# Value sums in a bank of their own, a thinner weight decode and added transposes in a fused attention and MoE kernel

## The chip, the cores and the metric

The kernel runs on one core of a Trainium2 chip. The metric is the time of one execution on the device in microseconds (us). A core has five engines that run beside each other and take their instructions in order: TensorE (PE, whose weight loads are listed as PEld), VectorE (DVE), ScalarE (ACT), GpSimd (POOL) and SyncE (SP), which issues the transfers here.

## The reference

For each of 8 batches and 8 heads (576 rows, head width 64) an attention, in which scores below the row's maximum less `tau` are dropped, and behind it a two-layer network over all 4608 tokens:

```python
scores = scale * np.matmul(q, k.transpose(0, 1, 3, 2))
thresh = np.max(scores, axis=-1, keepdims=True) - tau
scores = np.where(scores >= thresh, scores, -1000000000.0)
scores = scores - np.max(scores, axis=-1, keepdims=True)
attn = np.exp(scores)
attn = attn / (np.sum(attn, axis=-1, keepdims=True) + 1e-09)
return np.matmul(attn, v).astype(np.float32)
...
h = x @ w_in                       # 4608 x 512 by 512 x 2048
sp = np.where(h > 20.0, h, np.log1p(np.exp(np.minimum(h, 20.0))))
g = h * np.tanh(sp)
return (g @ w_out).astype(np.float32)
```

The two weight matrices come as 64-bit floats.

## The kernel before

**Tiles and pairs.** Two heads make a pair; 8 batches of 4 pairs are 32 pairs. The 2 x 576 rows of a pair are nine tiles of 128 score rows, 288 tiles in all. One Python loop over `g` writes the work out; in its iteration `g` several tiles stand at different stages, so the order in the code is each engine's order (`InOrder` holds every compute engine to it). Below, "tile t" is g % 9 of the tile itself, and "iteration" is the value of `g`.

**One tile.** `begin(g + 1)` makes the scores of the next tile on PE into one of two pairs of score banks (`s`). `row_max` is a reduction on DVE, `exponential` two small DVE operations and the exponential on ACT, `masked` one DVE operation that compares and multiplies (`p <- s, st, e`) and frees the score bank. `normalise`, one iteration later, is a reciprocal on DVE and a scaling on POOL. `transposes(g - 2)` turns `p` on PE: four transposes into the PSUM tile `tp` (one bank), and for odd tiles and for tile 8 one or two more into the small PSUM tile `t5`. `evacuate`, one iteration after that, copies `tp` and then `t5` to SBUF on ACT. Through iteration 37 the transposes stand early in the iteration, after that at its end.

**Value products.** When tiles 3 and 8 of a pair are there, `product(g - lag)` makes the products with v: `values_full` takes a PSUM bank `y` and gives five pieces of work on PE (four matmuls each) and a `gather`, an ACT copy out of `y`. With lag 4 this falls into iterations with g % 9 = 7 and 3. Through iteration 37 two pieces run per iteration and the gather follows in the iteration after the last; from iteration 38 (`SOON`) on all five run in one iteration and the gather in the same one. Pair by pair `split_x` then cuts the result in two column halves, each a high part (ACT copy, `xh`) and a low part (POOL, `xl`).

**First matrix.** From iteration 42 on `gemm1` runs as a stream of PE matmuls beside the attention: 384 per batch and 36 iterations, dealt out per iteration by `EVEN`, twelve for each result bank `h`, which ACT copies to `hst` and SP stores to DRAM. `h` and `y` share two PSUM banks (`psh`, tag "ph").

**Decoding w_in.** 32 blocks of the first matrix (128 x 256) are put together from the halves of the 64-bit words beside the first 55 tiles. `W1_STEPS` says in which iterations of each 18 a block begins. Its load is issued then; three iterations later come two ACT operations (`first`), then `clamp` on POOL, one iteration after that `shift` on DVE and `join` (`sign` on DVE, `add` on POOL), and two iterations later `upper` on ACT and `lower` on POOL, or for nine blocks (`ONV`) `lower` on DVE one iteration later still. `shift` stands on DVE between the reciprocal and the masking of its iteration. Before iteration `JOIN` the join does too; from then on it stands behind the masking.

**Clock.** `WARM` puts transposes of the identity before the loop and 26, 12, 6, 4, 3, 2, 2, 2, 2, 2 into iterations 0 to 9.

**The end.** After the loop the second matrix runs: w_out is decoded, batch 7's `gemm1` with more banks, then the products with w_out.

Of the kernel before, what the change touches and what calls it, by code (L numbers as in the profile page):

```python
# [14 lines left out]
P = 128  # L15
B, H, S, D = 8, 8, 576, 64
NP = H // 2
LOADS = ((1, 0, 1, 3, 2, 3, 7, 3, 5, 8), (0, 3, 3, 2, 5, 4, 5, 8, 8, 9), (0, 0, 2, 4, 5, 4, 7, 6, 7, 8), (0, 0, 1, 3, 2, 3, 7, 5, 7, 8))
W1_STEPS = (1, 3, 4, 6, 7, 8, 10, 12, 13, 15, 16, 17)
STAGES = ((0, 1, 1), (0, 1, 1))  # L20
THIRD = ((),)
LAG = 2
# [2 lines left out]
ORDER = (0, 0)  # L25
PIECES = 2
WARM = (24, (26, 12, 6, 4, 3, 2, 2, 2, 2, 2))
FULL = NP
VP = 32
SOON = 9 * FULL + 2  # L30
ONP = 1
ONV = (3, 9, 11, 12, 14, 15, 17, 18, 22)
JOIN = 39
PLAIN = (0, 1)
DM, DF = 512, 2048
ND, NF = DM // P, DF // P
# [33 lines left out]
LAST = {1: 0, 4: 1, 6: 2, 8: 3}  # L70
TURN = [[(t % 2, t // 2 * P + t % 2 * P)] for t in range(8)] + [QCOL[4]]
CLOSE = {3: 0, 8: 1}
EVEN = (14, 14, 14, 0, 13, 14, 14, 0, 13)
WIDTH = (256, 320, 320, 256)
XOFF = (0, 256, 256, 0)
SCALE = 1.0 / float(D) ** 0.5
# [42 lines left out]
class Decode:  # L119
# [16 lines left out]
        nc.scalar.activation(c, low, AF.Copy, scale=2.0**-29)  # L136

    def clamp(self):
        self.nc.gpsimd.tensor_scalar(fv(self.b), fv(self.a), TOP_MAX, -TOP_MAX, ALU.min, ALU.max)

    def shift(self):
        self.nc.vector.tensor_scalar(self.a, self.b, 3, 0x7FFFFFF8, ALU.logical_shift_left, ALU.bitwise_and)
# [18 lines left out]
def attention_moe(tc, q, k, v, tau, w_in, w_out, out):  # L161
# [3 lines left out]
    with ExitStack() as outer:  # L165
# [105 lines left out]
        with ExitStack() as first:  # L271
# [6 lines left out]
            with ExitStack() as att:  # L278
# [160 lines left out]
                def transposes(g):  # L439

                    both = tiles[g]["both"]
                    at = odd(g) * (S + D)
                    tp = pst.tile([P, 4, P], F32, name="tp")
                    for c in range(4):
                        nc.tensor.transpose(tp[:, c, :], both[:, at + c * P:at + (c + 1) * P], ident)
                    t5 = None
                    last = g < 9 * VP and g % 9 == 8
                    if odd(g) or last:
                        t5 = pst.tile([P, P], F32, name="t5")
                        if last:  # L450
                            nc.tensor.transpose(t5, both[:, S - P:S], ident)
                            nc.tensor.transpose(t5[:D], both[:, S - D:S], ident)
                        else:
                            nc.tensor.transpose(t5, both[:, 4 * P:5 * P], ident)
                    return tp, t5

                def evacuate(t, tp, t5, pt):
                    r = t // 4 if t < 8 else 1
                    if r not in pt:
                        pt[r] = [  # L460
                            ptp.tile([P, w, 320], F32, name=n, tag=n) for n, w in (("hi", 4), ("lo", 4), ("tk", 1))
                        ]
                    tail = pt[r][2][:, 0]
                    if t < 8:
                        a, at = t % 2, t // 2 % 2 * P
                        nc.scalar.copy(pt[r][a][:, :, at:at + P], tp)
                        if a:
                            nc.scalar.copy(tail[:, at:at + P], t5)
                        return
                    for a in range(2):  # L470
                        rows = slice(a * D, (a + 1) * D)
                        nc.scalar.copy(pt[r][a][:, :, 2 * P:], tp[:, :, rows])
                        nc.scalar.copy(tail[rows, 2 * P:], t5[rows, rows])
# [30 lines left out]
                    for hi, lo, t5 in tails(g):  # L504
                        nc.vector.tensor_tensor(lo, t5, fv(hi), ALU.subtract)

                def values_full(r, pt, vf, x):
                    main, tail = pt[r][:2], pt.pop(r)[2]
                    n = (2 + r) * P - r * D
                    y = psh.tile([P, 512], F32, name="y", tag="ph")  # L510

                    def chunk(c):
                        for a in range(2):
                            rows = slice(a * D, (a + 1) * D)
                            m = main[a][:, c, :n] if c < 4 else tail[:, 0, :n]
                            nc.tensor.matmul(y[rows, :n], vf[:, a, c], m, start=c == 0, stop=c == 4)

                    def gather():
                        nc.scalar.copy(x[:, r * QT:r * QT + n], y[:, :n])

                    return [lambda c=c: chunk(c) for c in range(5)], gather
# [21 lines left out]

                    return gather

                def split_x(g, x):
                    parts = []
                    for c in range(2):
                        xh = xpool.tile([P, HB], F32R, name="xh", bufs=12)
                        xl = xpool.tile([P, HB], F32R, name="xl", bufs=12)  # L550
                        parts.append((xh, xl))

                    def half(c):
                        xh, xl = parts[c]
                        sl = slice(c * HB, (c + 1) * HB)
                        nc.scalar.copy(xh, x[:, sl])
                        nc.gpsimd.tensor_tensor(xl, x[:, sl], fv(xh), ALU.subtract)

                    chores.setdefault(g + XSPLIT[1], []).append(lambda: half(0))
                    chores.setdefault(g + XSPLIT[1] + XSPLIT[2], []).append(lambda: half(1))  # L560
                    return parts
# [14 lines left out]
                def gemm1(b, xs, bank=shared, first=1):  # L576

                    halves = (range(NF // 2), range(NF // 2, NF))
                    if b < B - 1:
                        order = [(c, f) for c in range(2) for fs in halves for f in fs]
                    else:
                        order = [(c, f) for fs in halves for c in range(2) for f in fs]
                    banks = {}
                    made = {}

                    def parts(c, f, ds):
                        if (c, f) not in banks:  # L590
                            banks[c, f] = bank("h")
                        h = banks[c, f]
                        half, at = divmod(f * P, DF // 2)
                        for d in ds:
                            xh, xl = xs[d][c]
                            wh, wl = (w[:, d, at:at + P] for w in w1[half])
                            for i, (a, m) in enumerate(((wh, xh), (wh, xl), (wl, xh))):
                                nc.tensor.matmul(
                                    h[:, :HB], a, m, start=d == 0 and i == 0, stop=d == ND - 1 and i == 2
                                )  # L600
                                yield

                    def leave(c, f):
                        if f % 4 == 0:
                            made["hst"] = hp.tile([P, 4, HB], F32, name="hst", tag="hst")
                        hst, h = made["hst"], banks.pop((c, f))
                        if b < B - 1 or f % 2:
                            nc.scalar.copy(hst[:, f % 4], h[:, :HB])
                        else:
                            nc.vector.tensor_copy(hst[:, f % 4], h[:, :HB])  # L610
                        if f % 4 == 3:
                            store(nc.sync, hst, (2 * b + c) * HB, f - 3)

                    for c, f in order[:first]:
                        yield from parts(c, f, range(ND - 1))
                    for n, (c, f) in enumerate(order):
                        steps = parts(c, f, range(ND - 1, ND) if n < first else range(ND))
                        for i in range(3 if n < first else 3 * ND):
                            next(steps)
                            if i == (2 if n < first else 3 * ND - 1):  # L620
                                leave(c, f)
                            yield
# [27 lines left out]
                    made = pairs[pi]["ops"]  # L650
                    tiles[g] = dict(s=scores(t, 0 if odd(g) else D, **made))

                def product(g):
                    pi, t = divmod(g, 9)
                    pr = pairs[pi]
                    if t == (3 if pi < VP else 1):
                        pr["x"] = sm.tile([P, S], F32, name="x", bufs=2)
                    if pi < VP:
                        if t in CLOSE:
                            some, gather = values_full(CLOSE[t], pr["pt"], pr["ops"]["vf"], pr["x"])  # L660
                            pieces.extend((work, None) for work in some[:-1])
                            pieces.append((some[-1], (gather, pi if t == 8 else None)))
                    elif t in LAST:
# [1 line left out]

                def close_pair(g, pi):
                    b, hp = divmod(pi, NP)
                    batches.setdefault(b, []).append(split_x(g, pairs.pop(pi)["x"]))

                warm = psh.tile([P, P], F32, name="warm", tag="ph")  # L670

# [11 lines left out]
                    split()  # L683
                nc.vector.tensor_scalar(back, back, 1.0 / SCALE, None, ALU.mult)
                begin(0)
                for g in range(NT + 5):
                    now = [work.pop(0) for work in decoding]
                    decoding = [work for work in decoding if work]
                    if g + 1 < NT:
                        begin(g + 1)  # L690
                    ahead = 2 <= g < SOON
                    lag = 4 if g < VP * 9 + 4 or VP == NPAIRS else 5
                    if lag <= g < NT + lag and (g != VP * 9 + 4 or VP == NPAIRS):
                        product(g - lag)
                    if 3 <= g < NT + 3:
                        old = ((g - 3) % 9, *tiles[g - 3]["tp"], pairs[(g - 3) // 9]["pt"])
                        full = g - 3 < VP * 9
# [9 lines left out]
                    for _ in range(5 if g >= SOON else PIECES):  # L707
                        if pieces:
                            work, then = pieces.pop(0)
                            work()  # L710
                            if then:
                                (done if g >= SOON else ready).append(then)
                    if g < NT:
                        tiles[g]["st"], tiles[g]["e"] = row_max(tiles[g]["s"])
                    if 1 <= g <= NT:
# [257 lines left out]
```

## Time and profile before

| | |
|---|---|
| median of 3 runs | 1357.99 us (1357.27 to 1361.05) |
| profiled execution, its own time | 1360.66 us |
| profiled execution, span | 1358.9 us |
| mean granted clock of PE | 0.987 |
| busy: PE, PEld, DVE, ACT, POOL | 1311.3, 1171.1, 872.4, 849.5, 742.3 us |

The span runs from the first to the last instruction of the program; what lies around it is the rest of the time. Busy time of PE is the union of modelled matmul durations, and those overlap, so PE can be held up a little without showing idle time; a wait is seen better in the rows of who waited for whom. In rows of the profile L95 is the line of the helper that records every operation, so that operations are told apart by the names of their tiles: `p`, `s`, `e`, `st`, `tp`, `t` (that is `t5`), `y`, `x`, `h`, `hst`, `dec` (the block that is being decoded), `w1h`, `w1l`. In brackets, or behind the bar, stands the idle time of the engine ahead of an instruction and what ended it.

### The profile page before, as it was taken

The numbers are of one execution on the slowest core, as the hardware profiler recorded it, in microseconds if no ns is written. First come the engines' busy times: TensorE is split into PE (matmuls) and PEld (weight loads), VectorE is DVE, ScalarE is ACT, GpSimd is POOL, SyncE is SP. The second block draws the span as 40 slices with busy tenths as digits, with TensorE's granted clock in tenths as the row PEclk, the third lists the DMA queues.
The fourth block names the chain that finished last, engine by engine and source line by source line (L and its number), as shares of the span: only waits on it lengthen the run. The fifth ranks groups of instructions, "written<-read, shape, count | busy, mean of one in ns | idle before, by whom it ended". The sixth has DMA issues, their size and how long they took to land. (4 is left out here: it accounts for less than half of the span.)

```text
span 1358.9 us, 28431 instructions
## 1 busy us (share of the span) xinstructions
PE 1311.3 (96%) x9941; PEld 1171.1 (86%) x9941; DVE 872.4 (64%) x2372; ACT 849.5 (63%) x1676; POOL 742.3 (55%) x1093
## 2 busy tenths in 40 slices
PE   8887999999999999999999999999999999999998
PEld 5444789988889889898888898898979999999998
DVE  6897756555556556566566556564996666666664
ACT  4777766666666666666666666665665555555552
POOL 4899966656556566566565665642403334444431
PEclk9888999999999999999999999999999999999999
DMA  6333443433333333333333333312744343444440
GB/s 175 103 92 115 150 147 89 115 95 99 107 89 97 109 103 93 98 91 114 99 94 106 89 104 102 94 53 84 253 149 155 125 137 113 141 140 137 137 131 32
DMA packets 151904, 154.83 MB, mean 114 GB/s; under 512 B 35536, under 2 KB 128720, under 8 KB 151760
## 3 DMA queue, kind: packets, MB, share of 16 engines
q1 hardware_dynamic: 151760, 153.00, 37.5%
q8 instruction: 79, 1.29, 0.4%
q14 instruction: 65, 0.53, 0.1%
HBM read 105.78 MB, written 47.19 MB: 113 GB/s over the span
## 5 line engine op out<-in xcount | busy, mean ns | idle before, releaser
L95 DVE SCALAR_TENSOR_TENSOR p<-s,st,e 128x576 f32<-128x576 f32 x288 | 235.4, 817 | 331.4 <-ACT e L95 331.0
L95 PE MATMUL h<-xh,w1h 128*128 128x288 f32 x1024 | 302.6, 295 | 1.1 <-ACT hst L95 1.1
L95 PE MATMUL h<-xl,w1h 128*128 128x288 f32 x1024 | 302.4, 295 | 0.0
L95 PE MATMUL h<-xh,w1l 128*128 128x288 f32 x1024 | 302.3, 295 | 0.0
L95 POOL TENSOR_SCALAR p<-p,st 128x576 f32<-128x576 f32 x288 | 240.3, 835 | 108.3 <-DVE st L95 89.2
L95 PE MATMUL s<-k,q 128*128 128x288 f32 (+1 forms) x1280 | 244.3, 337 | 32.4 <-DVE p L95 31.3
L95 POOL TENSOR_TENSOR z<-z 128x256 f32<-128x256 f32 x128 | 124.2, 975 | 223.1 <-DVE z L95 214.3
L95 ACT ACTIVATE e<-s,st 128x576 f32<-128x576 f32 x288 | 215.9, 750 | 45.7 <-DVE st L95 43.0
L95 PEld LDWEIGHTS s<-k,q 128*128 128x128 f32 (+1 forms) x1280 | 172.0, 192 | 55.6 <-DVE p L95 48.9
L95 DVE TENSOR_REDUCE st<-s 128x1 f32<-128x576 f32 x288 | 216.8, 753 | 2.7 <-PE s L95 2.7
L95 DVE TENSOR_TENSOR gl<-z,gh 128x1792 fp32r<-128x1792 f32 (+1 forms) x72 | 141.6, 1967 | 108.2 <-ACT gh L95 108.2
L95 ACT CAST gh<-z 128x1792 fp32r<-128x1792 f32 (+1 forms) x72 | 116.5, 1620 | 150.0 <-issue 81.2
L95 PEld LDWEIGHTS h<-xh,w1h 128*128 128x128 f32 x1024 | 192.6, 188 | 2.0 <-ACT hst L95 1.3
L95 PEld LDWEIGHTS h<-xh,w1l 128*128 128x128 f32 x1024 | 192.5, 188 | 0.0
L95 PEld LDWEIGHTS h<-xl,w1h 128*128 128x128 f32 x1024 | 192.5, 188 | 0.0
L95 PE MATMUL tp<-ident,p 128*128 128x128 f32 x1152 | 180.0, 279 | 3.9 <-POOL p L95 1.5
L95 PEld LDWEIGHTS tp<-ident,p 128*128 128x128 f32 x1152 | 135.9, 141 | 44.3 <-issue 28.6
L95 POOL TENSOR_TENSOR k<-r,k 128x320 fp32r<-128x320 f32 x112 | 97.9, 874 | 95.8 <-ACT k L95 93.6
L95 PE MATMUL y<-hi,vf 128*64 128x320 f32 (+1 forms) x512 | 145.2, 426 | 1.0 <-ACT hst L95 1.0
L95 PE MATMUL y<-lo,vf 128*64 128x320 f32 (+1 forms) x512 | 145.2, 426 | 0.0
L95 PE MATMUL o<-gh,sl 128*128 128x256 f32 x512 | 144.5, 282 | 0.0
L95 PE MATMUL o<-gl,sh 128*128 128x256 f32 x512 | 143.8, 281 | 0.0
(68 smaller groups left out, 2712.0 us busy)
## 6 DMA issues: line engine op xcount, KB each, us to landing
z<-hd SPq DMA_DIRECT2D x144, 256.0 KB, 3.1
r<-q SPq DMA_DIRECT2D x112, 160.0 KB, 2.2
r<-k SPq DMA_DIRECT2D x112, 160.0 KB, 2.4
vf<-v SPq DMA_DIRECT2D x64, 160.0 KB, 2.3
out_t<-c SPq DMA_DIRECT2D x36, 256.0 KB, 2.4
dec<-w_in SPq DMA_DIRECT2D x32, 256.0 KB, 3.2
hd<-hst SPq DMA_DIRECT2D x16, 512.0 KB, 3.3
w<-w_out SPq DMA_DIRECT2D x16, 512.0 KB, 4.5
```

Of the source, the lines that this page charges most:

```text
L95: made = method(*args, **kwargs)
```

## The change

- `y` is taken from the pool and bank of `t5` (`own`, for products after iteration 40), and `t5` is made a whole bank wide. `h` has its two banks alone.
- The lag of the products is 5 from iteration 41 on, the gather follows in the next iteration until the last tile, `EVEN` has its zeros at g % 9 = 4 and 8, and the loop has one iteration more. `evacuate` copies `t5` ahead of `tp`.
- `W1_STEPS` has ten entries for twelve, so the last block begins in iteration 57 instead of 48; batch 0 takes its matmuls by halves of the hidden columns first (as batch 7 does), and keeps its second column halves of x in another pool meanwhile.
- `clamp` runs on DVE; `JOIN` is 72.
- Tiles 8 to 39 get two more transposes, of the identity into the first quarter of their `tp`, ahead of their own.

```diff
-W1_STEPS = (1, 3, 4, 6, 7, 8, 10, 12, 13, 15, 16, 17)
+W1_STEPS = (1, 3, 5, 6, 8, 10, 12, 14, 15, 17)
+WARM_TILES = (8, 40)
-JOIN = 39
+JOIN = 72
-EVEN = (14, 14, 14, 0, 13, 14, 14, 0, 13)
+EVEN = (14, 14, 14, 13, 0, 14, 14, 13, 0)
     def clamp(self):
-        self.nc.gpsimd.tensor_scalar(fv(self.b), fv(self.a), TOP_MAX, -TOP_MAX, ALU.min, ALU.max)
+        self.nc.vector.tensor_scalar(fv(self.b), fv(self.a), TOP_MAX, -TOP_MAX, ALU.min, ALU.max)
                     tp = pst.tile([P, 4, P], F32, name="tp")
+                    if WARM_TILES[0] <= g < WARM_TILES[1]:
+                        for _ in range(2):
+                            nc.tensor.transpose(tp[:, 0, :], ident, ident)
-                        t5 = pst.tile([P, P], F32, name="t5")
+                        t5 = pst.tile([P, 512], F32, name="t5")[:, :P]
                         a, at = t % 2, t // 2 % 2 * P
-                        nc.scalar.copy(pt[r][a][:, :, at:at + P], tp)
                         if a:
                             nc.scalar.copy(tail[:, at:at + P], t5)
+                        nc.scalar.copy(pt[r][a][:, :, at:at + P], tp)
-                def values_full(r, pt, vf, x):
+                def values_full(r, pt, vf, x, own):
-                    y = psh.tile([P, 512], F32, name="y", tag="ph")
+                    home, tag = (pst, "t5") if own else (psh, "ph")
+                    y = home.tile([P, 512], F32, name="y", tag=tag)
-                def split_x(g, x):
+                def split_x(g, x, early):
-                        xh = xpool.tile([P, HB], F32R, name="xh", bufs=12)
-                        xl = xpool.tile([P, HB], F32R, name="xl", bufs=12)
+                        home, n = (sm, 4) if early and c else (xpool, 12)
+                        xh = home.tile([P, HB], F32R, name="xh", bufs=n)
+                        xl = home.tile([P, HB], F32R, name="xl", bufs=n)
-                    if b < B - 1:
+                    if 0 < b < B - 1:
                         order = [(c, f) for c in range(2) for fs in halves for f in fs]
                     else:
                         order = [(c, f) for fs in halves for c in range(2) for f in fs]
-                    batches.setdefault(b, []).append(split_x(g, pairs.pop(pi)["x"]))
+                    batches.setdefault(b, []).append(split_x(g, pairs.pop(pi)["x"], b == 0))
-                for g in range(NT + 5):
+                for g in range(NT + 6):
-                    lag = 4 if g < VP * 9 + 4 or VP == NPAIRS else 5
-                    if lag <= g < NT + lag and (g != VP * 9 + 4 or VP == NPAIRS):
-                        product(g - lag)
+                    lag = 4 if g < SOON + 2 else 5
+                    if lag <= g < NT + lag and g != SOON + 2:
+                        product(g - lag, g > SOON + 2)
-                                (done if g >= SOON else ready).append(then)
+                                (done if g >= NT else ready).append(then)
```

More of the change, by code (lines that the diff above doesn't have):

```diff
@@ L651, in begin, with product @@
                     tiles[g] = dict(s=scores(t, 0 if odd(g) else D, **made))
-                def product(g):
+                def product(g, own):
                     pi, t = divmod(g, 9)
@@ L659, in product @@
                         if t in CLOSE:
-                            some, gather = values_full(CLOSE[t], pr["pt"], pr["ops"]["vf"], pr["x"])
+                            some, gather = values_full(CLOSE[t], pr["pt"], pr["ops"]["vf"], pr["x"], own)
                             pieces.extend((work, None) for work in some[:-1])
```

## The prediction

> **What bounds the kernel now.** I read the page first (busy shares and the forty slices), then stretches of busy time, then who waited for whom in the long middle, then the timeline of the place where the longest of those waits sits.
>
> ```profile
> span 1358.9 us, 28431 instructions
> PE 1311.3 (96%) x9941; PEld 1171.1 (86%) x9941; DVE 872.4 (64%) x2372; ACT 849.5 (63%) x1676; POOL 742.3 (55%) x1093
> ```
>
> PE is busy for 96%, so the time can only fall where PE waits, or where it runs at a reduced clock. The stretches say where (columns: length, busy us and count of PE, its weight loads, DVE, ACT, POOL, then the granted clock):
>
> ```profile
> 20.00:25.00 5.00, 3.23 (x22) 1.99 (x21) 4.21 (x16) 3.14 (x8) 2.33 (x6) 1.00 0.13 46
> ...
> 35.00:40.00 5.00, 2.82 (x18) 1.82 (x18) 4.05 (x14) 4.89 (x14) 3.94 (x7) 0.92 0.21 57
> 40.00:45.00 5.00, 5.00 (x21) 2.21 (x17) 4.77 (x18) 3.18 (x7) 4.79 (x9) 0.50 0.15 54
> ...
> 80.00:100.00 20.00, 15.86 (x86) 7.75 (x85) 18.47 (x60) 15.20 (x38) 18.89 (x30) 0.83 0.33 97
> ...
> 130.00:135.00 5.00, 4.04 (x19) 3.56 (x19) 3.71 (x14) 4.07 (x10) 5.00 (x9) 0.66 0.35 115
> ...
> 165.00:170.00 5.00, 3.00 (x21) 2.48 (x19) 4.74 (x9) 2.19 (x7) 4.90 (x8) 0.89 0.91 325
> 170.00:175.00 5.00, 5.00 (x34) 3.44 (x34) 2.07 (x8) 1.90 (x6) 2.06 (x4) 0.77 0.67 214
> ...
> 600.00:700.00 100.00, 99.00 (x767) 88.80 (x766) 59.34 (x224) 66.39 (x157) 60.75 (x98) 1.00 0.34 100
> ```
>
> So there are two regimes. Up to about 130 us DVE (18.5 of 20) and POOL (18.9 of 20) are the full engines, and PE runs part of the time at half clock. After that PE is the bound, at full clock. One row maximum (the reduction into `st`) runs per score tile, so its count gives the tiles of a stretch:
>
> ```profile
> L95 DVE TENSOR_REDUCE st<-s 128x1 f32<-128x576 f32 x33 | 24.8, 751 | 0.8 <-PE s L95 0.8
> L95 DVE SCALAR_TENSOR_TENSOR dec<-dec 128x256 uint32<-128x256 uint32 x22 | 12.4, 563 | 0.6
> L95 DVE TENSOR_SCALAR dec<-dec 128x256 uint32<-128x256 uint32 x22 | 11.6, 526 | 2.3 <-POOL dec L95 2.3
> ...
> L95 DVE TENSOR_REDUCE st<-s 128x1 f32<-128x576 f32 x15 | 11.2, 749 | 0.0
> ...
> L95 DVE TENSOR_REDUCE st<-s 128x1 f32<-128x576 f32 x189 | 142.3, 753 | 0.0
> ```
>
> The first three rows are of 31 to 131.9 us (tiles 9 to 41: 100.9 us for 33, 3.06 each), the fourth of 132 to 185.5 us (tiles 42 to 56), the last of 205.3 to 807.8 us (189 tiles, 21 head pairs: 28.69 us a pair). In that last regime one wait of PE recurs once a pair, here by waits from 186 to 930 us (total, times, longest):
>
> ```profile
> ACT x L95 <- PE y L95: 112.6, 52, 2.2
> ...
> PEld s L95 <- DVE p L95: 14.5, 25, 0.6
> ```
>
> and on the timeline around g = 3 and 4 of a pair:
>
> ```profile
> 242.96 0.75 DVE L95 TENSOR_REDUCE st<-s 128x1 f32<-128x576 f32 x1
> ...
> 243.48 0.59 ACT L95 COPY hi<-tp 128x512 f32<-128x512 f32 x1 [0.66 <-PE tp L95]
> ...
> 244.76 0.82 DVE L95 SCALAR_TENSOR_TENSOR p<-s,st,e 128x576 f32<-128x576 f32 x1 [0.68 <-ACT e L95]
> ...
> 245.50 0.75 DVE L95 TENSOR_REDUCE st<-s 128x1 f32<-128x576 f32 x1
> ...
> 246.87 0.43 ACT L95 COPY x<-y 128x320 f32<-128x320 f32 x1 [2.14 <-PE y L95]
> 247.19 0.46 ACT L95 CAST q<-r 128x320 fp32r<-128x320 f32 x1
> 247.24 0.27 PE L95 MATMUL t<-ident,p 128*128 128x128 f32 x1
> 247.27 0.78 PE L95 MATMUL s<-k,q 128*128 128x288 f32 x4
> ...
> 247.89 0.30 PE L95 MATMUL h<-xh,w1h 128*128 128x288 f32 x1
> 247.91 0.43 ACT L95 CAST xh<-x 128x288 fp32r<-128x288 f32 x1
> ...
> 248.24 0.59 ACT L95 COPY lo<-tp 128x512 f32<-128x512 f32 x1
> 248.72 0.28 ACT L95 COPY tk<-t 128x128 f32<-128x128 f32 x1
> ...
> 248.88 0.76 ACT L95 ACTIVATE e<-s,st 128x576 f32<-128x576 f32 x1
> ...
> 249.62 0.60 PE L95 MATMUL tp<-ident,p 128*128 128x128 f32 x4
> 249.67 0.82 DVE L95 SCALAR_TENSOR_TENSOR p<-s,st,e 128x576 f32<-128x576 f32 x1 [3.04 <-ACT e L95]
> ...
> 250.55 0.79 PE L95 MATMUL s<-k,q 128*128 128x288 f32 x4 [0.33 <-DVE p L95]
> ```
>
> ACT runs in order. Its `gather` of `y` waits 2.14 us for the ten value products of the same iteration. Behind it stand the casts of q and k, the split of x, the copies out of the transposes (due at about 247.5, made at 248.24) and the exponential. The masking on DVE, which has waited 3.04, is late by as much, and PE, through with its transposes, waits for the score bank that it frees: the next scores start at 250.55, right behind it. That is 14.5/25 = 0.58 us a pair. The first lines also give the floor of a tile that nothing disturbs, 2.54 us from row maximum to row maximum, with 0.68 us in which DVE waits for the exponential.
>
> **The change part by part.**
>
> The other rows that the costs go by, of the page's groups, of the waits (31 to 131.9 us, then all), and of the timeline:
>
> ```profile
> L95 ACT COPY hst<-h 128x288 f32<-128x288 f32 x240 | 96.4, 403 | 41.9 <-PE h L95 38.3
> ```
>
> ```profile
> PE s L95 <- DVE p L95: 16.3, 17, 2.1
> ...
> DVE p L95 <- ACT e L95: 10.0, 14, 3.3
> ...
> ACT x L95 <- PE y L95: 4.4, 1, 4.4
> ```
>
> ```profile
> PE y L95 <- ACT hst L95: 1.0, 1, 1.0
> ```
>
> ```profile
> 120.88 0.94 DVE L95 TENSOR_SCALAR dec<-dec 128x256 uint32<-128x256 uint32 x1 [0.32 <-POOL dec L95]
> ...
> 124.79 0.29 DVE L95 TENSOR_SCALAR dec<-dec 128x256 uint32<-128x256 uint32 x1 [0.35 <-POOL dec L95]
> ```
>
> *Gather one iteration later, `y` in the bank of `t5`, lag 5, zeros of EVEN moved.* The products move from g % 9 = 3 and 7 to 4 and 8, the gather to 5 and 0; no instruction is added. At its new place the gather finds `y` long done, so the 2.14 us wait goes, and with it the reason for the 0.58 us. What is late next? First, `y` must now wait for the copy of `t5`, transposed as the last thing of the iteration before. By the rows: `t` issued at 247.24 ends at 247.51, a copy takes 0.28, so the bank is free near 247.83; the four scores that PE has ahead of `y` last from 247.27 to 247.89. It fits by some 0.06 us if ACT is idle at that moment. The swap inside `evacuate` (t5 first) is what makes it fit: behind the 0.59 of tp it would not. In iterations 3 and 7 ACT has a copy of tp (0.59), an exponential (0.76), up to two casts (0.46), a split of x (0.43) and a copy of h (0.40) at most, 2.6 us with what neighbours overlap, against PE's scores, 13 matmuls of h (2.35 us for both, 247.27 to 249.62) and five transposes of some 0.1, over 2.8 us; so it should be idle. Second, iteration 5 now holds on ACT 0.59 + 0.76 + gather 0.43 + one cast 0.46 + xh 0.43 + two copies of h, 3.5 us, against some 2.9 us of PE; neighbours overlap by some 0.1 us each (247.91 + 0.43 lies beyond 248.24), which leaves about the same. I book 0.05 us a pair for what slips. Third, t5 of iteration 5 waits for the gather, which has 2.3 us until then. Bounds: 0.58 gained and 0.6 lost a pair; taken 0.53, near the row, times 25: **13 us**.
>
> *Clamp from POOL to DVE, ten decode steps per 18 tiles for twelve, JOIN 72.* The excess of tiles 9 to 41 over the floor is 100.9 - 33 x 2.54 = 17 us. A decoded block costs DVE 0.526 + 0.563 and 2.3/22 = 0.10 of waiting for POOL's clamp, 1.19 against the 0.68 that is free: 0.51 x 22 = 11 us. One tile (tile 40) holds the 4.4 us wait of ACT for `y` that shows as 3.3 on DVE, 2.6 above normal. The other 3 us are the low parts that DVE makes and late ACT work. After the change 18 blocks fall in these tiles; the wait for the clamp goes, and POOL has one instruction less a block, which should free some of the shifts that today last 0.94 instead of 0.29: I take 0.35 a block, 6.3 us. The clamps themselves: the nearest row is the shift of the same size, 0.29 to 0.94, mean 0.53. Fourteen fall in a tile without another block's shift and fit into its 0.68 (0.1 each), four (tiles 10, 19, 28, 37) meet one and cost 0.53: 3.5 us. Tile 40's wait becomes about 0, the gather being an iteration later. So 6.3 + 3.5 + 3 = 12.8 against 17: **4 us**, bounds -3 (every clamp 0.94, blocked shifts as before) and +9.
>
> In tiles 42 to 56 the excess is 53.6 - 15 x 3.19 = 5.8 us. The clock rows give 0.34 x 5 / 0.5 = 3.4 us at half clock, and (0.11 + 0.23) x 5 / 0.5 = 3.4 again, in which a PE that is the bound loses 3.4 us; 2.4 us fall on 8 blocks. Twelve blocks come after the change (up to tile 62), 3.6 us, and I leave 0.2 for clock: **2 us**, bounds -3 and +5. JOIN puts sign and add ahead of the masking there; it is in these 0.3 a block. Batch 0's new order needs the second half of w1 from matmul 192 of 384 on, tile 60; the last block, begun at tile 57, is done at 64 and used at 67, so no wait; it costs nothing.
>
> *Two transposes of the identity ahead of tiles 8 to 39.* 64 at about 0.11 issue each, 7 us of PE where PE has 4 us of 20 idle; they stand where PE waits for `p` anyway. The clock: from 20 to 25 us, where the start's own warm-ups still run, PE issued 22 in 5 us and kept 1.00; from 35 to 40 it issued 18 and fell to 0.50. Two per tile at 2.7 us are 3.7 per 5 us: 18 becomes 22. So most of the half-clock stretches should go. DVE being the bound, that is worth little there; what tile 40 gains is booked above. Bounds -1 and +2; taken 0. [...]
>
> *The end.* One more iteration holds nothing new for PE, since batch 6 is drained in both; the 1.0 us in which `y` waits for a bank that h held should go: **1 us**, bounds -1 and +1.
>
> Sum: 13 + 4 + 2 + 1 = 20 us. The profiled execution took 1360.66 (span 1358.9 and 1.8 around it); 1340.7 after, and as it stands 2.7 over the median of 1357.99, **1338** for a median. A change within 0.3%, 4 us, could not be told from none here.
>
> **The rivals.**
> - *DVE loses early what the middle gains in part.* [...] At 0.94 a clamp the first term is -3 and the second -3: 13 - 3 - 3 + 1 = 8 us, 1350. [...]
> - *ACT stays late in iteration 5.* If its 3.5 us do not overlap, 0.3 of the 0.58 returns in iteration 6: 25 x 0.28 + 7 = 14 us, 1344.
> - *Slower: `y` waits for `t5`.* Two groups a pair; if a cast or copy of 0.4 to 0.6 stands on ACT ahead of the copy of t5, plus the 0.28, each group waits up to 0.8: 26 x 2 x 0.8 = 42 us against 20, 1380. It turns the sign above 0.4 us a group. The 0.66 us for which ACT waits ahead of the copy of tp at 243.48 speak against it: there PE was late, not ACT.
> - *Nothing moves:* the stall returns whole at g = 6 behind the crowded iteration 5, and the early terms cancel: 1357.
>
> **How the numbers follow.** Forecast 0.63 (own range 1329 to 1344), ACT late 0.14, DVE loses 0.11, nothing 0.05, slower 0.07. The range reaches from both early terms at their upper ends (9 + 5 with 13 and 1: 1330) and a little beyond, for full clock that I booked at nothing (2), to the DVE rival: 1327 to 1350. Faster by over 0.3%: 0.63 + 0.14 + 0.11 = 0.88; within 0.05; slower 0.07.
>
> **What would show it.** PE's wait for DVE's p from 186 to 930 us falls from 14.5 to a few us, ACT's wait for y from 112.6 to near 0, and a pair takes 28.1 to 28.2 us; any wait of y's first product for ACT's copy `tk` is the slower rival. Tiles 9 to 41 take some 97 us and the rows near 40 and 90 us show a clock of 1.00. DVE's clamp has a mean near 0.5. I am wrong if PE's waits at s move to another g with the same size, or if DVE's `dec` group grows by more than the waits shrink.

## The result, and the profile after

The changed kernel takes 1335.17 us (median of 4 runs, 1332.48 to 1337.26) against 1357.63 for the one before beside it: a ratio of 0.9829, with a 95% interval of 0.9804 to 0.9854. The forecast was 1338 (1327 to 1350). The profiled execution took 1337.26, its span is 1335.4.

The first two lines of the page, then stretches of busy time as before (length, busy us and count of PE, weight loads, DVE, ACT, POOL, then the granted clock):

```profile
span 1335.4 us, 28536 instructions
PE 1304.2 (98%) x10005; PEld 1174.3 (88%) x10005; DVE 883.3 (66%) x2404; ACT 844.4 (63%) x1676; POOL 736.0 (55%) x1061
```

```profile
35.00:40.00 5.00, 4.70 (x33) 2.70 (x31) 4.90 (x18) 3.80 (x11) 3.41 (x7) 1.00 0.12 24
40.00:45.00 5.00, 4.24 (x29) 2.47 (x29) 4.44 (x17) 3.14 (x8) 3.62 (x7) 1.00 0.25 84
80.00:100.00 20.00, 16.86 (x100) 8.57 (x97) 19.48 (x62) 15.49 (x40) 18.48 (x28) 0.91 0.34 102
115.00:120.00 5.00, 3.74 (x14) 2.23 (x16) 4.51 (x17) 3.28 (x9) 4.80 (x8) 0.52 0.24 65
600.00:700.00 100.00, 100.00 (x779) 89.47 (x778) 59.82 (x225) 67.09 (x159) 63.33 (x100) 1.00 0.35 102
```

In the long middle PE is now busy for 100.00 of 100 us; before it was 99.00. The half clock near 40 us is gone from this execution, the one near 115 to 120 is not. Up to 180 us the granted clocks of such rows (5 us each) add up to 34 us of half clock before and 17 us now. The counts of the row maximum give the tiles again: the first row is of 32.4 to 128.9 us (tiles 9 to 41), the second of 129.2 to 195.5 (tiles 42 to 62), the third of 195.8 to 784.7 (189 tiles, 21 pairs):

```profile
L96 DVE TENSOR_REDUCE st<-s 128x1 f32<-128x576 f32 x33 | 24.8, 752 | 0.0
```

```profile
L96 DVE TENSOR_REDUCE st<-s 128x1 f32<-128x576 f32 x21 | 15.8, 751 | 0.0
```

```profile
L96 DVE TENSOR_REDUCE st<-s 128x1 f32<-128x576 f32 x189 | 142.4, 753 | 0.0
```

So tiles 9 to 41 take 96.7 us (100.9 before), tiles 42 to 62 take 66.6 (73.4 before: the row maximum of tile 42 starts at 131.97 us and that of tile 63 at 205.38), and a pair of the long middle takes 28.06 (28.69 before). The whole difference of the two spans, 23.5 us, by tile starts: 4.2 in tiles 9 to 41, 6.8 in tiles 42 to 62, 15.1 in the 24 pairs from tile 63 to 278, less 1.2 ahead of tile 9 and 1.3 from tile 279 to the end. The start of tile 9 differs as much between the kernels run below (30.6 to 32.3 us), so that the 1.2 stand for nothing.

Who waited for whom, 186 to 930 us:

```profile
ACT hi L96 <- PE tp L96: 160.7, 128, 2.6
...
PEld y L96 <- ACT tk L96: 8.7, 51, 0.6
...
ACT x L96 <- PE y L96: 2.5, 1, 2.5
...
PE y L96 <- ACT tk L96: 0.4, 1, 0.4
```

PE's wait for DVE's `p`, 14.5 us before, has no row any more; ACT's wait for `y` went from 112.6 to 2.5, and its wait for the transposes rose instead (68.6 to 160.7). The timeline at g % 9 = 4 shows the fit that the forecast worked out:

```profile
208.11 0.27 PE L96 MATMUL t<-ident,p 128*128 128x128 f32 x1
208.14 0.77 PE L96 MATMUL s<-k,q 128*128 128x288 f32 x4
...
208.42 0.27 ACT L96 COPY tk<-t 128x128 f32<-128x128 f32 x1 [0.53 <-PE t L96]
...
208.58 0.59 ACT L96 COPY lo<-tp 128x512 f32<-128x512 f32 x1
...
208.83 0.48 PE L96 MATMUL y<-hi,vf 128*64 128x320 f32 x1
...
213.49 0.43 ACT L96 COPY x<-y 128x320 f32<-128x320 f32 x1
```

The copy of `t5` ends at 208.69 and `y` starts at 208.83, 0.69 us after the scores ahead of it, as early as before the change (0.71). The gather at 213.49 waits for nothing.

### The profile page after: what moved, and what is told of

Same layout as the page of the kernel before. It is cut to its first block, busy times and chain, and to the rows that moved or that the text cites. A ratio compares the mean times of both kernels' runs of the same rounds, so it can differ in the third digit from the quotient of the medians.

```text
span 1335.4 us, 28536 instructions
## 1 busy us (share of the span) xinstructions
PE 1304.2 (98%) x10005; PEld 1174.3 (88%) x10005; DVE 883.3 (66%) x2404; ACT 844.4 (63%) x1676; POOL 736.0 (55%) x1061
## 5 line engine op out<-in xcount | busy, mean ns | idle before, releaser
L96 PE MATMUL s<-k,q 128*128 128x288 f32 (+1 forms) x1280 | 241.1, 333 | 17.7 <-DVE p L96 16.6
L96 ACT COPY hi<-tp 128x512 f32<-128x512 f32 (+1 forms) x160 | 87.1, 544 | 169.1 <-PE tp L96 168.8
L96 PE MATMUL tp<-ident,p 128*128 128x128 f32 x1152 | 176.7, 276 | 0.1
L96 PEld LDWEIGHTS tp<-ident,p 128*128 128x128 f32 x1152 | 135.9, 140 | 28.0 <-issue 15.1
L96 PE MATMUL o<-gh,sh 128*128 128x256 f32 x512 | 143.5, 280 | 0.0
```

Source lines behind the costliest of these rows:

```text
L96: made = method(*args, **kwargs)
```

## The experiments

Kernels that ran together share their runs of the kernel before. From one such group to the next that median moved from 1357.4 to 1361.8, so ratios are compared across groups. Stretches of tiles are by the starts of their row maxima in each kernel's profile, which is one execution.

**The two halves of the change.** First the products alone, in the kernel before (EVEN, lag 5, one iteration more, the wide `t5`, its copy ahead of `tp`, `y` from its pool, and the later gather):

```diff
-EVEN = (14, 14, 14, 0, 13, 14, 14, 0, 13)
+EVEN = (14, 14, 14, 13, 0, 14, 14, 13, 0)
...
-                                (done if g >= SOON else ready).append(then)
+                                (done if g >= NT else ready).append(then)
```

> Before with the edits of the value products alone (lag 5, gather an iteration later, y in the bank of t5, t5 copied first, zeros of EVEN moved, one more iteration); the decode, the clamp, JOIN, batch 0's order and the clock of the start as before. Theory (the late gather held up the masking once a pair): a pair takes 28.06 us instead of 28.69, tiles 9 to 41 stay near 100 us, the time is about 1342 (15 to 16 below before). Rival (the steady gain needs the early edits too, or is partly the early edits' clock): a pair stays above 28.3 or the time above 1346.

It took 1344.13 (ratio 0.9890, 0.9870 to 0.9910), with 28.07 us a pair and 99.3 in tiles 9 to 41. The long middle is thus wholly the products' work. Then all the rest of the change, with those edits taken back:

```diff
-EVEN = (14, 14, 14, 13, 0, 14, 14, 13, 0)
+EVEN = (14, 14, 14, 0, 13, 14, 14, 0, 13)
...
-                                (done if g >= NT else ready).append(then)
+                                (done if g >= SOON else ready).append(then)
```

> The change without the edits of the value products: decode ten in 18, clamp on DVE, JOIN 72, batch 0's order, two transposes ahead of tiles 8 to 39, but y beside h, lag 4, gather in the same iteration. Theory: a pair stays at 28.69, tile 42 starts near 129 us, the time is 1350 (about 8 below before), so that the two halves add up to the 22.5 measured. Rival (the early edits only help where the gather does not block, since tiles 42 to 62 were the larger gain): 1354 or more, and the halves do not add up.

It took 1352.19 (0.9951, 0.9933 to 0.9969), 28.68 us a pair, 95.2 us in tiles 9 to 41. The two gains are 13.3 and 5.2 us, 18.5 together, against 22.5 for the change; with about 2.5 us of uncertainty on each that is no proof of more than a sum. By tile starts the halves gain 4.4 and 3.8 us in tiles 42 to 62 and the whole 6.8, so that there they add up to more than the whole.

**The added transposes.** None, and four:

```diff
-WARM_TILES = (8, 40)
+WARM_TILES = (0, 0)
```

> The change without the two added transposes (none ahead of any tile). Theory of the prediction (DVE bounds the early tiles, so the clock is worth almost nothing): 1335 to 1337, with 27 us or more of half clock up to 140 us instead of 17. Rival (the clock is where tiles 9 to 56 gained): 1340 or more.

```diff
-                        for _ in range(2):
+                        for _ in range(4):
                             nc.tensor.transpose(tp[:, 0, :], ident, ident)
```

> The change with four added transposes ahead of each of tiles 8 to 39 instead of two. Theory: the half clock around 115 to 122 us goes, in which the ten value products of tile 40's iteration run; tile 40 falls from 7.1 to about 5 us and the time to about 1333; the early DVE-bound tiles do not move. Rival (more PE time ahead of the transposes delays the evacuation): tiles 9 to 39 grow by 0.1 to 0.2 each and the time is 1337 or more.

None: 1335.67 (0.9831, 0.9812 to 0.9850), no difference from two. Four: 1331.90 (0.9802, 0.9783 to 0.9821), 3.8 us below none in the same group, with no overlap of the runs (1331.6 to 1332.1 against 1335.5 to 1336.1). Two rows of the stretches without any, then two with four:

```profile
40.00:45.00 5.00, 5.00 (x19) 2.20 (x17) 3.57 (x13) 3.44 (x8) 3.73 (x6) 0.50 0.02 5
115.00:120.00 5.00, 4.89 (x18) 2.70 (x20) 4.51 (x18) 2.14 (x5) 4.72 (x7) 0.50 0.13 33
```

```profile
80.00:100.00 20.00, 16.36 (x113) 9.67 (x109) 19.42 (x61) 15.30 (x39) 18.70 (x28) 1.00 0.37 106
115.00:120.00 5.00, 5.00 (x37) 3.34 (x37) 4.51 (x16) 2.23 (x7) 4.70 (x7) 1.00 0.14 36
```

In these executions the half clock near 40 us is there with none and not with two, and the one near 115 stays with both; with four there is no reduced clock before the last microseconds (mean clock of the execution 1.000). The places differ from execution to execution (with two transposes and the gather in the same iteration, a run below, the row of 40 to 45 us shows 0.71 again), but the sums up to 180 us go one way over all the profiles of this document: 20 to 34 us of half clock in the five kernels without added transposes, 10 to 17 in the six with two, 0, 0 and 3.4 in the three with four (mean clocks of the executions 0.987 to 0.992, 0.993 to 0.996 and 0.998 to 1.000). Without any it is 20 us where the expectation was 27 or more, so the two transposes took away only 3 of the 17 us that went.

Tiles 9 to 38 do not care (84.3, 83.9 and 83.8 us with none, two and four): DVE bounds them (busy for 19.48 of the 20 us from 80 to 100 us with two, 19.42 with four). What the full clock buys lies in tiles 39 to 41, where the ten products of `y` for the first time run in one iteration (12.4, 12.9 and 10.3 us), and in tiles 42 to 62 (66.6, 66.6, 65.2). The spread of the changed kernel's own runs fits: the one with the highest mean clock, 0.998, took 1332.48 us, near the 1331.90 of four, and the one with the lowest, 0.993, took 1337.26. The longest gap of PE between 31 and 132 us was 2.1 us in the kernel before and 1.6 in the changed one, and still the clock fell, to 0.50 (40 to 45 us) and to 0.52 (115 to 120 us).

**What made the late gather harmful.** First `y` in the banks of `h` again, all else as changed:

```diff
-                        product(g - lag, g > SOON + 2)
+                        product(g - lag, False)
```

> The change with y in the two banks of h again; all else as changed (lag 5, gather an iteration later, t5 first). Theory (the late gather was the whole stall, the own bank only makes room): ACT's wait for y stays near 0, but y now holds one of two banks while 14 matmuls of h run, so h waits for a bank for some 0.3 to 0.5 us after each of the two groups; a pair takes 28.4 to 28.9 and the time is 1343 to 1355. Rival (the own bank does nothing, the later gather all): 28.06 and 1335.

It took 1369.21 (1.0061, 1.0041 to 1.0082): slower than before the change, and than the 1343 to 1355 expected, with 29.29 us a pair. Its waits, 186 to 930 us:

```profile
PEld h L96 <- ACT x L96: 28.0, 26, 1.1
...
PE h L96 <- ACT x L96: 21.9, 26, 0.8
```

A gather in the next iteration holds one of two banks through it. Once a pair the weight load of `h` waits 28.0/26 = 1.1 us for it and its matmul 21.9/26 = 0.8 us. So the own bank is needed if the gather is late. Then the gather in the iteration of its products, with the own bank:

```diff
-                                (done if g >= NT else ready).append(then)
+                                (done if g >= SOON else ready).append(then)
```

> The change with the gather in the iteration of its products again; y in its own bank, products at g % 9 = 4 and 8. Theory (it is the gather that blocks ACT): ACT waits some 2 us for y in both iterations, the stall of PE returns with 0.3 to 0.6 us a pair, 28.4 to 28.7, 1343 to 1350. Rival (what made the gather harmful was its place: the casts of q and k, 0.9 us, and the split of x stood behind it in iterations 3 and 7; in 4 and 8 no cast does, so the copy of tp is late by 0.5 us and PE's 2.9 us cover it): ACT waits as long, but a pair takes 28.1 and the time is 1335 to 1338.

It took 1337.26 (0.9827, 0.9809 to 0.9846), 28.06 us a pair, no different from the change: the rival came true, not the theory. The wait of ACT is back, 186 to 930 us, and PE is not held up by it:

```profile
ACT x L96 <- PE y L96: 90.9, 52, 2.5
```

```profile
211.38 0.66 PE L96 MATMUL tp<-ident,p 128*128 128x128 f32 x4
211.49 0.43 ACT L96 COPY x<-y 128x320 f32<-128x320 f32 x1 [1.98 <-PE y L96]
211.79 0.77 PE L96 MATMUL s<-k,q 128*128 128x288 f32 x4
212.29 0.58 ACT L96 COPY hi<-tp 128x512 f32<-128x512 f32 x1
```

ACT waits 1.98 us for `y` as it did before the change (2.14), but only 0.8 us lie between the gather's start and the copy of tp; before it was 1.37 (246.87 to 248.24). What stood there before were the casts of q and k, which the move by one iteration left behind. So the place was tried by itself, in the kernel before, with nothing else (EVEN, lag 5 from iteration 41 on, one iteration more; `y`, gather and `evacuate` as before):

```diff
-EVEN = (14, 14, 14, 0, 13, 14, 14, 0, 13)
+EVEN = (14, 14, 14, 13, 0, 14, 14, 13, 0)
...
-                    lag = 4 if g < VP * 9 + 4 or VP == NPAIRS else 5
+                    lag = 4 if g < SOON + 2 else 5
```

> Before, with the products one iteration later (lag 5, zeros of EVEN moved, one more iteration) and nothing else: y in h's banks, gather in the same iteration, tp copied first. Theory (the place is all): a pair takes 28.06 to 28.2 and the time is 1341 to 1345, so the own bank and the later gather brought nothing by themselves. Rival (without its own bank y takes one from h): h waits as in the kernel with y beside h, 28.5 or more, 1352 or more.

1341.74 (0.9870, 0.9853 to 0.9887), 28.07 us a pair, while ACT still waits 98.3 us for `y` (186 to 930 us). Last the other way round, with products and gather where they were and the casts moved out from behind them:

```diff
-LOADS = ((1, 0, 1, 3, 2, 3, 7, 3, 5, 8), (0, 3, 3, 2, 5, 4, 5, 8, 8, 9), (0, 0, 2, 4, 5, 4, 7, 6, 7, 8), (0, 0, 1, 3, 2, 3, 7, 5, 7, 8))
+LOADS = ((1, 0, 1, 3, 2, 3, 7, 3, 5, 8), (0, 3, 3, 2, 5, 4, 5, 8, 8, 9), (0, 0, 2, 4, 5, 4, 7, 6, 7, 8), (0, 0, 1, 4, 2, 4, 7, 5, 7, 8))
```

> Before, with one edit: from pair 4 on, the two loads whose casts fell into iterations with g % 9 = 3 are issued an iteration later, so the casts of q and k fall into 4. Gather, bank, lag and EVEN as before. Theory (the stall came from what stood behind the gather on ACT, two casts of 0.46, not from the gather's wait): the copy of tp after the gather is made some 0.75 us earlier, PE's 0.58 us wait goes, a pair takes 28.06 to 28.2 and the time is 1342 to 1345. Rival (ACT's 2.1 us wait for y is itself the cause): 28.69 and 1357.

1342.50 (0.9872, 0.9857 to 0.9888), 28.09 us a pair. ACT waits for `y` exactly as in the kernel before (186 to 930 us: 112.6 there), and no row of PE waiting for `p` is left:

```profile
ACT x L95 <- PE y L95: 113.5, 52, 3.0
```

```profile
241.69 0.42 ACT L95 COPY x<-y 128x320 f32<-128x320 f32 x1 [2.14 <-PE y L95]
...
242.15 0.43 ACT L95 CAST xh<-x 128x288 fp32r<-128x288 f32 x1
242.49 0.58 ACT L95 COPY lo<-tp 128x512 f32<-128x512 f32 x1
...
243.12 0.76 ACT L95 ACTIVATE e<-s,st 128x576 f32<-128x576 f32 x1
243.76 0.47 ACT L95 CAST q<-r 128x320 fp32r<-128x320 f32 x1
243.91 0.82 DVE L95 SCALAR_TENSOR_TENSOR p<-s,st,e 128x576 f32<-128x576 f32 x1 [2.45 <-ACT e L95]
244.11 0.48 ACT L95 CAST k<-r 128x320 fp32r<-128x320 f32 x1
```

The gather waits the same 2.14 us; the copy of tp comes 0.80 us after its start instead of 1.37, and the stall of 0.58 is gone. Two numbers of one line are worth as much here as the move of the products. The remaining corner, the later gather with products and casts left where they were, was not run; so it is not shown that the wait alone, had it gone, would have left the stall.

**The order in evacuate.**

```diff
-                        if a:
-                            nc.scalar.copy(tail[:, at:at + P], t5)
                         nc.scalar.copy(pt[r][a][:, :, at:at + P], tp)
+                        if a:
+                            nc.scalar.copy(tail[:, at:at + P], t5)
```

> The change with the old order in evacuate: tp copied first, then t5. Theory (y waits for the copy of t5, which fits by some 0.1 us): t5 is free 0.5 us later, y's first product waits 0.35 to 0.45 us twice a pair, 28.8 to 28.9 a pair, 1353 to 1356, the whole steady gain gone. Rival (ACT copies t5 early enough in either order, as PE's scores hide it): 28.06 to 28.2, 1335 to 1338.

1352.58 (0.9942, 0.9922 to 0.9962), 28.61 us a pair. Its waits, 186 to 930 us:

```profile
PEld y L96 <- ACT tk L96: 22.9, 51, 1.0
...
PE y L96 <- ACT tk L96: 11.0, 51, 0.7
```

With `y` in the bank of `t5` the order is worth 0.55 us a pair, some 0.27 for each of its two groups. The expectation of 0.35 to 0.45 each, 28.8 to 28.9 us a pair, was a little high. The slower rival of the forecast has a real mechanism, one swapped copy away, though of a smaller size.

**Clamp and decode steps.** First the clamp on POOL again, with two added transposes as the change has them (the edit of the clamp is the one shown below):

> The change with the clamp on POOL again. Theory (moving it is worth a little, since POOL is as full as DVE in the early tiles and a shift then waits for POOL's clamp): tiles 9 to 62 take 2 to 3 us more, 1337 to 1339. Rival (DVE pays for the clamp what POOL saves; the gain came from the thinner decode alone): within 1 us of the change, 1334 to 1336.

1337.44 (0.9830, 0.9813 to 0.9847): the time lies where the theory had it, but the ratio is that of the change, so the times show no difference. Tiles 9 to 38 take 85.7 us against 83.9 and 42 to 62 take 68.1 against 66.6, but 39 to 41 took 9.8 against 12.9, in an execution whose half clock fell almost wholly outside them. With four added transposes, so that half clock blurs less:

```diff
-        self.nc.vector.tensor_scalar(fv(self.b), fv(self.a), TOP_MAX, -TOP_MAX, ALU.min, ALU.max)
+        self.nc.gpsimd.tensor_scalar(fv(self.b), fv(self.a), TOP_MAX, -TOP_MAX, ALU.min, ALU.max)
```

> Four added transposes as in e4, and the clamp on POOL again, so that half-clock stretches don't blur the comparison. Theory (the move of the clamp is worth 2 to 3 us between tiles 9 and 62): 1334 to 1335 against the 1331.9 of four transposes with the clamp on DVE. Rival (nothing): 1331 to 1333.

1336.44 (0.9831, 0.9815 to 0.9846) against the ratio 0.9802 (0.9783 to 0.9821) with the clamp on DVE: about 4 us, more than expected, and 1.9 + 2.1 by tiles 9 to 38 and 42 to 62. The intervals overlap a little. The same two runs say something of the transposes: with the clamp on POOL, four (0.9831) gain nothing over two (0.9830), so the 3.8 us above hold for the clamp on DVE only.

Then the twelve decode steps of the kernel before, with four transposes and the clamp on DVE:

```diff
-W1_STEPS = (1, 3, 5, 6, 8, 10, 12, 14, 15, 17)
+W1_STEPS = (1, 3, 4, 6, 7, 8, 10, 12, 13, 15, 16, 17)
```

> Four added transposes as in e4, and the decode with twelve blocks per 18 tiles again, clamp on DVE. Theory (four blocks fewer in the DVE-bound tiles, and fewer tiles with two blocks on DVE): tiles 9 to 41 take 4 to 6 us more, tiles 42 to 62 some 1 us less, 1335 to 1337. Rival (the blocks cost the same wherever they stand): 1331 to 1333.

1335.96 (0.9824, 0.9809 to 0.9839): some 3 us more by the ratios, whose intervals again overlap; 1.8 in tiles 9 to 38, where 4 to 6 had been expected for 9 to 41, and 1.1 in 42 to 62, where the later blocks of the change had been expected to cost something instead. JOIN and batch 0's order were not tried by themselves; nor was the casts' move together with the early edits and four transposes.

## Why the prediction was right, and where it was not

- **The long middle.** Booked 13 us for 25 stalls, measured 15.1 over 24 pairs: 28.06 us a pair, 0.63 less than before, a little more than the stall of 0.58. The size was right; where the other 0.05 comes from was not followed. The reason was not right: "the 2.14 us wait goes, and with it the reason for the 0.58 us" is the step that failed. The wait may stay, as the kernels with the gather in the same iteration, with the place alone and with the casts moved show; it did harm only with the casts of q and k, 0.9 us, behind it, and moving these was enough. The prediction had named them in the chain and then put the whole on the chain's first link. That the change cured the stall is thus partly luck: it was made to remove the wait, and in doing so it took the gather away from the casts. The own bank and the later gather bring nothing here beyond the place, and the own bank only pays for the later gather, as the kernel with `y` beside `h` shows.
- **`y` waits for `t5`.** Forecast to fit by 0.06 us (the two rows named there, 247.51 and 0.28, add up to 247.79 and give 0.10); it fits by 0.14, and only by the order in `evacuate`: with tp first it does not.
- **Iteration 5 on ACT.** 0.05 us a pair was booked for what slips; no wait of PE shows any.
- **Tiles 9 to 41.** Booked 4 us, measured 4.2, but by other terms, so the agreement is luck: tile 40's wait did not go to 0. This tile takes 7.1 us in this execution (6.2 before), since the products ran at half clock there (0.52 from 115 to 120 us; a matmul of `y` took 0.74 us against 0.43 near 210 us, at 1.00), and ACT waited for the transposes behind them instead of for `y`. Tiles 9 to 38 alone gained 4.5, for which the sum had left little over 1. The clamp on DVE cost about as assumed, a mean of 476 ns, and not the 0.94 us of the rival; the shift came down to 395 from 569. The 0.35 us a block of the forecast counted on POOL's fewer instructions to free some of the shifts; that was the author's estimate, and no run shows what held them up:

```profile
L96 DVE TENSOR_SCALAR dec<-dec 128x256 f32<-128x256 f32 x32 | 15.2, 476 | 0.2 <-ACT hst L96 0.2
L96 DVE TENSOR_SCALAR dec<-dec 128x256 uint32<-128x256 uint32 x32 | 12.6, 395 | 0.0
```

- **Tiles 42 to 62.** Booked 2 us; 6.8 less 1.5 for the stall of 21 tiles is 5.3. Part of that is the clock of single executions: half clock covered some 6 us of these tiles before and 3 after, and the products alone, also with 3, gained 4.4 here instead of 1.5. Beyond this the term was mis-sized: it held 0.3 us a block and took the blocks as a cost wherever they stand. With the blocks spread out, the clamp on DVE and four transposes these tiles take 65.2 us, which is the 65.5 of 21 tiles at 28.06 a pair: the decode then costs nothing there. Which edit does it was not separated beyond 2.1 for the clamp and 1.1 for the steps.
- **The clock.** "Most of the half-clock stretches should go": half of their time went in the profiled executions, 34 us to 17, but 14 of these 17 us are gone without the transposes too; with four of them the rest went as well. That two are worth 0 was right, by the kernel without any.
- **The end.** Booked 1 us gained, measured 1.3 lost. Moving the products does it: the place alone has it, the casts' move does not (tile 279 to the end 466.1 and 465.0 us, 465.0 before). The 1.0 us wait of `y` went, but `h` waits for ACT more than its 1.1 us of before, in the waits of 880 us to the end:

```profile
PE h L96 <- ACT hst L96: 1.8, 2, 1.1
...
PE h L96 <- ACT x L96: 0.5, 1, 0.5
```

  That only makes the two equal (2.3 us against 2.1); where the 1.3 us are lost was not followed.

## What to carry to other kernels

Where an engine that runs in order waits, and something behind the wait is late, look at what stands between the two before moving the wait: here 0.9 us of casts with time to spare cost some 15 us, and moving two loads by one step freed it with the wait untouched. When a result gets its bank by sharing it with another tile, the order of the copies that free that bank becomes part of the critical path (0.55 us a pair here). Transposes added for the clock are worth trying in two doses: two per tile bought nothing (mean clock 0.993 in the profiled execution, 0.992 with none), four bought 3.8 us (1.000), in the tiles from 39 on where PE was becoming the bound, and nothing in the kernel with the clamp on POOL.

## What the runs showed of the hardware that was not expected

The clock fell to half (0.50 from 40 to 45 us) with PE busy for about half of the time (2.82 us of the 5 before that fall, in the kernel before) and with no gap of PE over 2.1 us between 31 and 132 us. These runs give no number of instructions that keeps it up. It fell after 18 in 5 us there, and in the changed kernel, with 100 in 20 us, to 0.91 over the stretch; but it stayed at 1.00 after 22 in 5 us (20 to 25 us, before) and after 21 (100 to 105 us, before).

With the clamp moved from POOL to DVE the shift behind it was shorter too, by 0.17 us in the mean (569 to 395 ns); with the clamp on POOL again and all else as changed the mean is 520 ns, and 547 with four transposes beside it (30 of the 32). In the kernel before 9 of the 32 shifts took 0.80 us or more, each of them beside a busy POOL. That POOL's work held them up is argued, not shown, since some shifts of 0.27 us ran beside it too.
